# Two small edits to a fused attention and feed-forward kernel: another home for the parts of g, and a last result in two halves

## The chip, the cores and the metric

The kernel runs on one core of a Trainium2 chip. A core has five engines that run side by side, each with its own queue: TensorE (PE, matrix products, with a weight load shown as PEld), VectorE (DVE), ScalarE (ACT), GpSimd (POOL) and SyncE (SP, which here only issues DMA transfers). The metric is the device time of one execution in microseconds (us), the median of three runs.

## The reference

Attention over 8 batches, 8 heads, 576 positions and head size 64, with a local mask (32 wide) in four heads and a strided mask in the other four; its output, 4608 tokens by 512, goes through a feed-forward layer with softplus and 2048 inner columns. All in float32.

```python
attn = softmax(where(mask, q @ k.T / 8, -1e9))        # per batch and head
x = (attn @ v) laid out as (4608, 512)
h = x @ w_in                                          # (4608, 2048)
g = np.maximum(h, 0.0) + np.log1p(np.exp(-np.abs(h)))
out = g @ w_out                                       # (4608, 512)
```

## The kernel before

The feed-forward layer takes nearly all of the time. To keep float32 accuracy with PE's single-pass kind of float32 (`F32R`), each operand is kept as a rounded high part and a low part that holds the rest; a product is then three matmuls: high by high, high by low, low by high. So x is held as the tiles `x_h` and `x_l`, the inner activation g as `gh` and `gl`, and each weight tile `w_i` (of w_in) and `w_o` (of w_out) has both parts side by side.

The 4608 tokens are worked off in 9 chunks c of 512, and the 2048 inner columns in 16 steps f of 128. For each (c, f) there are two groups of PE work, of 12 matmuls each, every one 128x128 by 128x512:

- `hidden` (line 607): ph <- x, w_i. The stationary operand is a 128x128 cut of w_i, the moving one 512 columns of x_h or x_l. All 12 add up in one PSUM bank `ph`.
- `output` (line 647): py <- w_o, g. The stationary operand is a 128x128 cut of gh or gl, the moving one 512 columns of w_o. There are four results `py0` to `py3`, one for each 128 tokens of the chunk, with three matmuls each per step; they add up over the 16 steps.

Between the two stands the softplus: ACT makes u from ph (lines 619, 622, 624), DVE adds the positive part (L628), rounds u to gh (L256, in `copy_on`) and subtracts to get gl (L640). `output` runs two steps behind `hidden`, so PE alternates: 12 matmuls of ph, 12 of py, and so on. Where the attention of later batches comes due, its small matmuls (L328 scores, L484 weighted sums) are put between the groups. The first 130 us or so hold the loads, the preparation of the weights and the first attention pairs.

The order on every engine is fixed when the program is built: a list of names written by hand (`FIRST`) for the beginning, then a planner (`Plan`) that lays tasks on engines by costs and wished-for times. Buffers come from pools. Each pool gets a fixed stretch of the on-chip memory SBUF, in the order in which the pools are opened, and a tile has the same byte place in each of the 128 partitions. The pool `g` holds three buffers each for gh and gl, 2048 bytes per partition each; the pool `st` holds four small tiles for the softmax, 160 bytes each; `io` holds four buffers that the results o pass through on the way out.

At the end of a chunk `result` (lines 655 to 659) copies each py out of PSUM into an `io` buffer (py0 and py2 on ACT, py1 and py3 on DVE) and SP stores it with one DMA of 256 KB.

Of the kernel before, what the change touches and what calls it, by code (L numbers as in the profile page):

```python
# [9 lines left out]
F32 = mybir.dt.float32  # L10
# [9 lines left out]
P = 128  # L20
# [59 lines left out]
class Plan:  # L80
# [8 lines left out]
    def add(self, name, urgency, engine, cost, fn, after=(), late=0.0):  # L89
        self.tasks[name] = (urgency, len(self.tasks), engine, cost, fn, after, late)  # L90
# [29 lines left out]
def attention_softplus_ffn(  # L120
# [9 lines left out]
    nc = tc.nc  # L130
    B, NPAIR, _, _, S = qk.shape
    D = P // 2
    NT, DM = out.shape
    DFF = w_in.shape[1]
    NCC = DM // P
    NFC = DFF // P
# [9 lines left out]
    START = [sum(CH[:c]) for c in range(NCHUNK)]  # L146
    TPC = max(CH) // P

    const = ctx.enter_context(tc.tile_pool(name="const", bufs=1))
    x_pool = ctx.enter_context(tc.tile_pool(name="x", bufs=1))  # L150
    w_pool = ctx.enter_context(tc.tile_pool(name="w", bufs=1))
    st_pool = ctx.enter_context(tc.tile_pool(name="st", bufs=4))
    u_pool = ctx.enter_context(tc.tile_pool(name="u", bufs=2))
    g_pool = ctx.enter_context(tc.tile_pool(name="g", bufs=3))
    io_pool = ctx.enter_context(tc.tile_pool(name="io", bufs=4))
    ps_s = ctx.enter_context(tc.tile_pool(name="ps_s", bufs=1, space=bass.MemoryType.PSUM))
    ps_o = ctx.enter_context(tc.tile_pool(name="ps_o", bufs=1, space=bass.MemoryType.PSUM))
# [39 lines left out]
    py = [ps_y.tile([P, DM], F32, name=f"py{t}") for t in range(TPC)]  # L197
# [57 lines left out]
    def copy_on(engine, dst, src):  # L255
        (engine.copy if engine is nc.scalar else engine.tensor_copy)(dst, src)  # L256
# [167 lines left out]
    def prob_transposes(n, quarters=range(4)):  # L424
        p = prob[n % 2]
        for quarter in quarters:
            for place, h in (divmod(quarter, 2),):
                src = p[64 * place + 32 * h : 64 * place + 32 * h + 32]
                for lo, hi in ((0, 6), (6, 9)):
                    a, i = block_at(lo, place)  # L430
                    for c in range(2):
                        nc.vector.transpose(  # L432
                            pt[
                                32 * (i + c) : 32 * (i + c) + 32,
                                h,
                                a : a + hi - lo,
                                32 * i : 32 * i + 32,
                            ],
                            src[:, lo:hi, 32 * c : 32 * c + 32],
                        )  # L440
# [157 lines left out]
    def hidden(c, f, pairs=range(NPAIR)):  # L598
        n = CH[c]
        if 0 in pairs:  # L600
            phs[c, f] = ps_h.tile([P, 512], F32, tag="ph", name=f"ph_{c}_{f}")[:, :n]
        ph = phs[c, f]
        t0 = START[c] % RING
        i = 3 * pairs[0]
        for cc in (PAIRS[pair] for pair in pairs):
            for half, x in ((0, "h"), (1, "h"), (0, "l")):
                nc.tensor.matmul(  # L607
                    ph,
                    lhsT=w32["i", f][:, half, cc * P : (cc + 1) * P],
                    rhs=x_of(x, cc)[:, t0 : t0 + n],  # L610
                    start=(i == 0),
                    stop=(i == 3 * NCC - 1),
                )
                i += 1

    def log_part(c, f, steps=range(3)):
        if 0 in steps:
            us[c, f] = u_pool.tile([P, 512], F32, tag="u", name=f"u_{c}_{f}")[:, : CH[c]]
            nc.scalar.activation(us[c, f], phs[c, f], AF.Abs)  # L619
        u = us[c, f]  # L620
        if 1 in steps:
            nc.scalar.activation(u, u, AF.Exp, scale=-1.0)  # L622
        if 2 in steps:
            nc.scalar.activation(u, u, AF.Ln, bias=1.0)  # L624

    def softplus(c, f):
        u = us[c, f]
        nc.vector.scalar_tensor_tensor(  # L628
            u, in0=phs.pop((c, f)), scalar=0.0, in1=u, op0=ALU.max, op1=ALU.add
        )  # L630

    def g_high(c, f, engine=nc.vector):
        g = g_pool.tile([P, 512], F32R, tag="gh", name=f"gh_{c}_{f}")[:, : CH[c]]
        ghs[c, f] = g
        copy_on(engine, g, us[c, f])

    def g_low(c, f, engine):
        g = g_pool.tile([P, 512], F32R, tag="gl", name=f"gl_{c}_{f}")[:, : CH[c]]
        gls[c, f] = g
        engine.tensor_tensor(g, us.pop((c, f)), ghs[c, f].bitcast(F32), op=ALU.subtract)  # L640

    def output(c, f, ts=None):
        gh, gl = ghs[c, f], gls[c, f]
        for t in ts or range(CH[c] // P):
            sl = slice(t * P, (t + 1) * P)
            for n, (g, half) in enumerate(((gh, 0), (gh, 1), (gl, 0))):
                nc.tensor.matmul(  # L647
                    py[t],
                    lhsT=g[:, sl],
                    rhs=w32["o", f][:, half],  # L650
                    start=(f == 0 and n == 0),
                    stop=(f == NFC - 1 and n == 2),
                )

    def result(c, t, engine):
        o = io_pool.tile([P, DM], F32, tag="io", name=f"o_{c}_{t}")
        copy_on(engine, o, py[t])
        t0 = START[c] + t * P
        nc.sync.dma_start(out[t0 : t0 + P, :], o)

    idle = ps_s.tile([P, 512], F32, tag="ps", name="idle")

# [80 lines left out]
    for t in range(4):  # L743
        task(f"y{t}", result, 0, t, of(f"y{t}", (nc.scalar, nc.vector)[t % 2]))
# [19 lines left out]
    steps = [(c, f) for c in range(NCHUNK) for f in range(NFC)]  # L764
# [7 lines left out]
    def joint(i):  # L772
        return pair_at.get(i, 0) > 2 * NPAIR
# [3 lines left out]
    t = 0.0  # L777
# [6 lines left out]
    add = plan.add  # L784
# [6 lines left out]
    for i in range(begin, len(steps) + LAG):  # L791
        if i < len(steps):
            c, f = steps[i]
            w, x = CH[c] / 384, when[i]
            after = [f"F{i-1}", f"u{i-2}"] + wanted.get(c, [])
            if joint(i - 1):
                after.append(f"L{pair_at[i - 1] - 1}1")
            add(f"F{i}", x, "PE", 2.1 * w, lambda c=c, f=f: hidden(c, f), after)
            after = [f"F{i}", f"l{i-2}"]
            add(f"A{i}", x + 2, "ACT", 1.5 * w, lambda c=c, f=f: log_part(c, f), after)  # L800
            add(f"u{i}", x + 3.7, "DVE", 0.55 * w, lambda c=c, f=f: softplus(c, f), [f"A{i}"])
            after = [f"u{i}", f"O{i-3}"]
            add(f"h{i}", x + 4.1, "DVE", 0.35 * w, lambda c=c, f=f: g_high(c, f), after)
            after = [f"h{i}", f"O{i-3}"]
            add(f"l{i}", x + 4.3, "DVE", 0.55 * w, lambda c=c, f=f: g_low(c, f, nc.vector), after)
        k = i - LAG
        c, f = steps[k]
        w = CH[c] / 384
        x = when[i] + 2.1 * w
        nt = CH[c] // P  # L810
        if 0 < f < NFC - 1:
            add(f"O{k}", x, "PE", 2.1 * w, lambda c=c, f=f: output(c, f), [f"l{k}", f"O{k-1}"])
            continue
        before = f"O{k-1}"
        for t in range(nt):
            name = f"O{k}" if t == nt - 1 else f"O{k}.{t}"
            after = [f"l{k}", before] + ([f"y{k-1}.{t}"] if f == 0 else [])
            add(name, x + 0.01 * t, "PE", 0.7, lambda c=c, f=f, t=t: output(c, f, (t,)), after)
            before = name
            if f == NFC - 1:  # L820
                e, cost, engine = (("ACT", 0.5, nc.scalar), ("DVE", 0.6, nc.vector))[t % 2]
                fn = lambda c=c, t=t, engine=engine: result(c, t, engine)
                add(f"y{k}.{t}", x + 0.7 * t + 0.7, e, cost, fn, [name])
# [5 lines left out]
    for i, n in pair_at.items():  # L829
        x = when[i]  # L830
# [16 lines left out]
        y = x + 1.5  # L847
# [17 lines left out]
        for j in range(4):  # L865
            name = f"P{n}" if j == 3 else f"P{n}.{j}"
            fn = lambda n=n, j=j: prob_transposes(n, (j,))
# [6 lines left out]
        for half in range(2):  # L874
# [8 lines left out]
            fn = lambda n=n, half=half: x_part(n, half, False)  # L883
            add(f"H{n}{half}", z, "ACT", 0.35, fn, after)
            fn = lambda n=n, half=half: x_part(n, half, True)
# [82 lines left out]
```

## Time and profile before

| | |
|---|---|
| time, median of 3 runs | 913.67 us (913.51 to 913.80) |
| the profiled execution's own time | 914.04 us |
| its span, first to last instruction | 912.0 us |
| mean clock granted to PE | 0.999 |
| busy: PE, DVE, ACT, POOL | 900.4, 601.9, 446.3, 60.1 us |

The profiled execution is 0.37 us longer than the median, and 2.0 us of its time lie outside the span. A row of the chain of work ("pieces") gives a start, a duration and how many instructions were taken together. A row of the instructions in order of time gives start, duration, engine, line, operation, what is written and read, and in brackets the idle time before. Matmuls overlap, and the ends shown are modelled, so the pace of PE is read from starts: from one row's start to another's, divided by the matmuls that lie between.

### The profile page before, as it was taken

The page shows a single profiled execution, that of the slowest core. Times are in us where ns is not written, and L with a number is a line of the kernel's source. Part 1 is how long each engine was busy: PE and PEld are TensorE (multiplying, and loading weights), DVE is VectorE, ACT ScalarE, POOL GpSimd, SP SyncE. Part 2 cuts the span into 40 slices and gives each one's busy share as a digit, 9 for nine tenths or more (in the row PEclk, how much of TensorE's full clock was granted, in tenths as well). Part 3 has the DMA queues.
Part 4 walks back from the last instruction along what each step waited for, and adds up shares of the span by engine and source line. Part 5 has one row for each costly group of instructions (what it writes and reads, how often), then busy time and mean ns, then how long its engine had stood idle before and what let it go on. Part 6 is the DMA issues. An engine that isn't in the chain of part 4 may idle for free.

```text
span 912.0 us, 14487 instructions
## 1 busy us (share of the span) xinstructions
PE 900.4 (99%) x5700; PEld 725.3 (80%) x5700; DVE 601.9 (66%) x1308; ACT 446.3 (49%) x795; POOL 60.1 (7%) x77
## 2 busy tenths in 40 slices
PE   8899999999999999999999999999999999999998
PEld 5677778888888888888888888888888888888886
DVE  7999997877767667766766676776776333333332
ACT  7898855445444444444544444445443333333332
POOL 4343540000000000000000000000000000000000
PEclk9999999999999999999999999999999999999999
DMA  9927212122211112111211121111200010001001
GB/s 339 349 102 246 81 30 73 43 57 67 70 39 43 43 44 89 32 42 43 89 44 43 43 78 27 42 43 43 89 18 17 1 46 1 1 1 47 0 1 47
DMA packets 49939, 58.27 MB, mean 64 GB/s; under 512 B 3152, under 2 KB 35024, under 8 KB 49872
## 3 DMA queue, kind: packets, MB, share of 16 engines
q1 hardware_dynamic: 49728, 57.16, 19.5%
q8 instruction: 45, 0.74, 0.3%
q10 hardware_dynamic: 144, 0.20, 0.1%
q14 instruction: 22, 0.18, 0.1%
HBM read 47.91 MB, written 9.44 MB: 63 GB/s over the span
## 4 chain that ended last, share of the span: by engine, by line
PE 90%; DVE 6%; ACT 1%; DMA 1%; issue 1%; POOL 0%; SPq 0%; ACTq 0%; DVEq 0%; POOLq 0%
PE py L647 42%; PE ph L607 41%; PE ps L328 3%; PE pv L484 2%; PE po L484 1%; DVE pt L432 1%; PE po L328 1%; DVE u L628 1%; DMA kT<-in_qk_dram 1%; DVE a_o L561 1%; DVE a_i L561 0%; ACT prob L374 0%; DMA raw_q<-in_qk_dram 0%; DVE a_o L578 0%; DVE a_i L578 0%
## 5 line engine op out<-in xcount | busy, mean ns | idle before, releaser
L647 PE MATMUL py<-w_o,gh 128*128 128x512 f32 x1152 | 365.7, 398 | 0.0
L607 PE MATMUL ph<-x_h,w_i 128*128 128x512 f32 x1152 | 358.8, 392 | 0.4 <-DVE u L628 0.4
L619 ACT ACTIVATE u<-ph 128x512 f32<-128x512 f32 x144 | 86.3, 600 | 409.0 <-PE ph L607 409.0
L647 PEld LDWEIGHTS py<-w_o,gh 128*128 128x128 f32 x1152 | 214.4, 188 | 51.8 <-POOL w_o L593 0.9
L607 PEld LDWEIGHTS ph<-x_h,w_i 128*128 128x128 f32 x1152 | 215.8, 188 | 48.9 <-DVE u L628 0.9
L647 PE MATMUL py<-w_o,gl 128*128 128x512 f32 x576 | 227.1, 394 | 0.0
L607 PE MATMUL ph<-x_l,w_i 128*128 128x512 f32 x576 | 225.9, 392 | 0.0
L628 DVE SCALAR_TENSOR_TENSOR u<-ph,u 128x512 f32<-128x512 f32 x144 | 98.9, 688 | 181.0 <-ACT u L624 179.2
L432 DVE STREAM_TRANSPOSE pt<-prob 32x192 f32<-32x192 f32 x448 | 137.1, 314 | 6.4
L647 PEld LDWEIGHTS py<-w_o,gl 128*128 128x128 f32 x576 | 108.6, 189 | 25.7
L607 PEld LDWEIGHTS ph<-x_l,w_i 128*128 128x128 f32 x576 | 108.1, 188 | 25.3
L640 DVE TENSOR_TENSOR gl<-u,gh 128x512 fp32r<-128x512 f32 x138 | 96.1, 697 | 11.2 <-ACT gh L256 0.3
L622 ACT ACTIVATE u<-u 128x512 f32<-128x512 f32 x144 | 91.0, 632 | 4.5
L624 ACT ACTIVATE u<-u 128x512 f32<-128x512 f32 x144 | 90.8, 631 | 4.4
L256 ACT COPY qT<-prob 64x576 f32<-64x576 f32 x56 | 70.6, 1260 | 0.3
L256 DVE CAST gh<-u 128x512 fp32r<-128x512 f32 x130 | 55.4, 426 | 10.6 <-PE py L647 0.5
L391 DVE TENSOR_TENSOR prob<-ps,mask_b 128x384 f32<-128x384 f32 x24 | 13.4, 558 | 53.6 <-PE ps L328 53.6
L328 PEld LDWEIGHTS ps<-kT,qT 128*64 128x64 f32 x720 | 23.6, 137 | 11.7 <-issue 8.8
L328 PE MATMUL ps<-kT,qT 128*64 128x64 f32 x720 | 28.0, 226 | 0.3 <-ACT qT L256 0.3
L484 PE MATMUL pv<-pt,v_in 128*64 128x96 f32 x396 | 22.2, 248 | 0.0
L422 DVE TENSOR_TENSOR prob<-prob,st 128x576 f32<-128x576 f32 x28 | 21.2, 758 | 0.9
L391 DVE TENSOR_TENSOR prob<-po,mask_b 128x192 f32<-128x192 f32 x24 | 8.6, 358 | 19.3 <-ACT x_h L522 19.3
(89 smaller groups left out, 516.7 us busy)
## 6 DMA issues: line engine op xcount, KB each, us to landing
out_dram<-o SPq DMA_DIRECT2D x36, 256.0 KB, 2.2
v_in<-in_v_dram SPq DMA_DIRECT2D x28, 320.0 KB, 3.7
ri<-in_moe_w_in_dram SPq DMA_DIRECT2D x16, 512.0 KB, 7.2
ro<-in_moe_w_out_dram SPq DMA_DIRECT2D x16, 512.0 KB, 7.7
prob<-in_qk_dram SPq DMA_DIRECT2D x28, 288.0 KB, 2.8
kT<-in_qk_dram SPq DMA_DIRECT2D x28, 288.0 KB, 3.0
v_in<-in_v_dram SPq DMA_DIRECT2D x28, 48.0 KB, 2.8
room<-in_v_dram SPq DMA_DIRECT2D x4, 320.0 KB, 7.2
```

The source lines that it names most:

```text
L256: (engine.copy if engine is nc.scalar else engine.tensor_copy)(dst, src)
L328: nc.tensor.matmul(ps[64 * place : 64 * place + 64, 64 * (x - lo) : 64 * (x - lo) + 64], lhsT=blocks_of(n)[:, c // 32].rearrange("p h l -> ...
L391: nc.vector.tensor_tensor(pv, sv, m, op=ALU.add)
L432: nc.vector.transpose(pt[32 * (i + c) : 32 * (i + c) + 32, h, a : a + hi - lo, 32 * i : 32 * i + 32,], src[:, lo:hi, 32 * c : 32 * c + 32],)
L484: nc.tensor.matmul(po[64 * h : 64 * h + 64, TILE * x : TILE * x + TILE], lhsT=vs[n][:, a, h, :], rhs=pt_of(n, a)[:, h, a % 2], start=True, ...
L607: nc.tensor.matmul(ph, lhsT=w32["i", f][:, half, cc * P : (cc + 1) * P], rhs=x_of(x, cc)[:, t0 : t0 + n], start=(i == 0), stop=(i == 3 * N ...
L619: nc.scalar.activation(us[c, f], phs[c, f], AF.Abs)
L622: nc.scalar.activation(u, u, AF.Exp, scale=-1.0)
L624: nc.scalar.activation(u, u, AF.Ln, bias=1.0)
L628: nc.vector.scalar_tensor_tensor(u, in0=phs.pop((c, f)), scalar=0.0, in1=u, op0=ALU.max, op1=ALU.add)
L640: engine.tensor_tensor(g, us.pop((c, f)), ghs[c, f].bitcast(F32), op=ALU.subtract)
L647: nc.tensor.matmul(py[t], lhsT=g[:, sl], rhs=w32["o", f][:, half], start=(f == 0 and n == 0), stop=(f == NFC - 1 and n == 2),)
```

## The change

The pool `g` is opened first instead of after `u`. And the very last result, py3 of the last chunk, is copied in two halves of 256 columns: DVE takes the first, ACT the second. The first half is stored through SP as before, the second through ACT's own DMA queue. Since each call of `result` takes an `io` buffer, the last chunk now takes five of the four.

```diff
+    g_pool = ctx.enter_context(tc.tile_pool(name="g", bufs=3))
     const = ctx.enter_context(tc.tile_pool(name="const", bufs=1))
     x_pool = ctx.enter_context(tc.tile_pool(name="x", bufs=1))
     w_pool = ctx.enter_context(tc.tile_pool(name="w", bufs=1))
     st_pool = ctx.enter_context(tc.tile_pool(name="st", bufs=4))
     u_pool = ctx.enter_context(tc.tile_pool(name="u", bufs=2))
-    g_pool = ctx.enter_context(tc.tile_pool(name="g", bufs=3))
     io_pool = ctx.enter_context(tc.tile_pool(name="io", bufs=4))
...
-    def result(c, t, engine):
-        o = io_pool.tile([P, DM], F32, tag="io", name=f"o_{c}_{t}")
-        copy_on(engine, o, py[t])
+    def result(c, t, engine, cols=slice(0, DM)):
+        o = io_pool.tile([P, DM], F32, tag="io", name=f"o_{c}_{t}")[:, cols]
+        copy_on(engine, o, py[t][:, cols])
         t0 = START[c] + t * P
-        nc.sync.dma_start(out[t0 : t0 + P, :], o)
+        queue = nc.scalar if engine is nc.scalar and cols.start else nc.sync
+        queue.dma_start(out[t0 : t0 + P, cols], o)
...
-            if f == NFC - 1:
+            if k == len(steps) - 1 and t == nt - 1:
+
+                for h, (e, engine) in enumerate((("DVE", nc.vector), ("ACT", nc.scalar))):
+                    cols = slice(DM // 2 * h, DM // 2 * (h + 1))
+                    fn = lambda c=c, t=t, engine=engine, cols=cols: result(c, t, engine, cols)
+                    add(f"y{k}.{t}{h}", x + 0.7 * t + 0.7, e, 0.35, fn, [name])
+            elif f == NFC - 1:
```

What the first edit does to the byte places, as the two programs have them (first byte of a pool in each partition; the last two columns say where a place stands within 512 bytes):

| pool | before | after | before, modulo 512 | after, modulo 512 |
|---|---|---|---|---|
| g (gh and gl, 2048 bytes each) | 208768 | 256 | 384 | 256 |
| const | 256 | 12544 | 256 | 256 |
| x (x_h, x_l, 6144 bytes each) | 23808 | 36096 | 256 | 256 |
| w (w_i, w_o, 4096 bytes each) | 72960 | 85248 | 256 | 256 |
| st (four tiles, 160 bytes apart) | 204032 | 216320 | 256 | 256 |
| u | 204672 | 216960 | 384 | 384 |
| io | 221056 | 221056 | 384 | 384 |

All pools from const to u move up by 12288 bytes, which is 24 times 512. The cuts that PE reads start at multiples of 512 bytes within their tiles. The g buffers stood behind the four tiles of st, which take 640 bytes together, and so 128 bytes off the raster on which x and w stand; now they stand on it.

No engine's order changes before the last result. There, on ACT's queue, these are the last rows before the change (o are the `io` buffers, numbered by chunk and result; in brackets the counters waited for: DMAHW for a landed DMA, DVE, PE and Activation for engines):

```order
L624 ACTIVATE u_8_15_7852<-u_8_15_7852 128x512 [waits Activation_49]
L256 COPY o_8_0_7876<-py0_106 128x512 [waits DMAHW5_49,PE_49]
L256 COPY o_8_2_7888<-py2_108 128x512 [waits DMAHW7_49,DMAHW3_49,PE_49]
L963 UNCONDITIONAL_BRANCH
```

And these after it, from the same place on:

```order
L256 COPY o_8_0_7876<-py0_106 128x512 [waits DMAHW5_49,PE_49]
L256 COPY o_8_2_7888<-py2_108 128x512 [waits DMAHW7_49,DMAHW3_49,PE_49]
L256 COPY o_8_3_7897<-py3_109 128x256 [waits DMAHW1_49,DVE_49,Activation_49]
L660 DMA out_0_dram<-o_8_3_7897 128x256 [waits Activation_49]
L970 UNCONDITIONAL_BRANCH
```

ACT's half of py3 does not wait for PE. It waits for DVE, whose last counted work is the other half's copy, and for DMAHW1, the counter of the store of o_8_0, whose buffer it takes over.

SP's queue ends with these stores after the change; before, the last one was 128x512 and stood alone:

```order
L660 DMA out_0_dram<-o_8_0_7876 128x512 [waits DMAHW1_49,Activation_49]
L660 DMA out_0_dram<-o_8_1_7882 128x512 [waits DMAHW2_49,DVE_49]
L660 DMA out_0_dram<-o_8_2_7888 128x512 [waits DMAHW3_49,Activation_49]
L660 DMA out_0_dram<-o_8_3_7894 128x256 [waits DMAHW4_49,DVE_49]
L970 UNCONDITIONAL_BRANCH
```

The store of o_8_3 on SP has shrunk to half, and its other half has gone to ACT's queue.

## The prediction

> **What bounds the kernel now.** I read the page's engine line, then the chain of work that ended last, then the instructions in order of time.
>
> ```profile
> span 912.0 us, 14487 instructions
> PE 900.4 (99%) x5700; PEld 725.3 (80%) x5700; DVE 601.9 (66%) x1308; ACT 446.3 (49%) x795; POOL 60.1 (7%) x77
> ```
>
> PE is busy all the time, but matmuls overlap, so this says nothing of its pace. The chain from 129 us to the end is PE alone, but for a last copy; this is its row by line:
>
> ```profile
> by line: PE py L647 47.8%; PE ph L607 44.9%; PE ps L328 2.6%; PE pv L484 1.7%; PE po L484 1.5%; PE po L328 1.1%; DVE o L256 0.1%; issue 0.0%
> ```
>
> So whatever makes a py or ph matmul shorter there shortens the kernel by as much. How long is a group of 12? The chain around 715 us:
>
> ```profile
> 712.35 2.75 PE ph L607 x12
> 715.10 1.14 PE pv L484 x24
> 716.24 2.98 PE py L647 x12
> 719.22 2.73 PE ph L607 x12
> 721.95 2.80 PE py L647 x12
> 724.75 2.76 PE ph L607 x12
> 727.50 2.80 PE py L647 x12
> 730.30 2.76 PE ph L607 x12
> ```
>
> A py group takes 2.80, a ph group 2.76, though both have twelve matmuls of the same shape; and the ph group at 719 takes 2.73. The starts of PE's rows show where the difference lies:
>
> ```profile
> 719.06 0.62 PE L607 MATMUL ph<-x_h,w_i 128*128 128x512 f32 x2
> ...
> 721.10 0.62 PE L607 MATMUL ph<-x_h,w_i 128*128 128x512 f32 x2
> ...
> 721.79 0.64 PE L647 MATMUL py<-w_o,gh 128*128 128x512 f32 x2
> ...
> 724.58 0.62 PE L607 MATMUL ph<-x_h,w_i 128*128 128x512 f32 x2
> ...
> 725.27 0.62 PE L607 MATMUL ph<-x_h,w_i 128*128 128x512 f32 x2
> ...
> 725.97 0.62 PE L607 MATMUL ph<-x_h,w_i 128*128 128x512 f32 x2
> ...
> 726.65 0.62 PE L607 MATMUL ph<-x_h,w_i 128*128 128x512 f32 x2
> ```
>
> From 719.06 to 721.10 lie nine matmuls: 0.2267 us each, a clean pace. The twelve of py from 721.79 to 724.58 take 0.2325 each. The ph group behind them starts in the slow mode (0.69 and 0.70 for three) and gets to the clean pace later (0.68 for three from 725.97). At the clean pace twelve take 2.72. So a py group loses 0.08, and an ordinary ph group 0.04 at its start, by what py leaves behind.
>
> Why is py slow? Not by the neighbours: DVE worked in the clean stretch, as its rows in order of time show.
>
> ```profile
> 719.28 0.43 DVE L256 CAST gh<-u 128x512 fp32r<-128x512 f32 x1
> 719.74 0.69 DVE L640 TENSOR_TENSOR gl<-u,gh 128x512 fp32r<-128x512 f32 x1
> ```
>
> And in the last py groups both DVE and ACT stood idle from about 903.7 on; the rows of three engines, with the idle time before them in brackets:
>
> ```profile
> 903.68 0.62 PE L647 MATMUL py<-w_o,gh 128*128 128x512 f32 x2
> ...
> 905.77 0.64 PE L647 MATMUL py<-w_o,gh 128*128 128x512 f32 x2
> ...
> 905.97 0.59 ACT L256 COPY o<-py 128x512 f32<-128x512 f32 x1 [4.35 <-PE py L647]
> ...
> 906.67 0.69 DVE L256 COPY o<-py 128x512 f32<-128x512 f32 x1 [3.00 <-PE py L647]
> ```
>
> Nine matmuls in 2.09, 0.2322 each, with PE alone at work. Nor is it the change of PSUM bank after every third matmul, since ph, all in one bank, shows the same slow mode at 724.58. Nor the place of single w_o tiles: the groups at 721.95 and 727.50 read different ones at 2.80 each. What is left that all py have and no ph has: the stationary cuts come from g, which stands 128 bytes off the 512-byte raster on which x, w_i and w_o all stand. PE reads a moving stream and the next weights at once; I take it that the two disturb each other by where they lie relative to each other, that ph has a timing without disturbance into which it settles, and that py has none. This is inferred, not shown: no row has the same matmul with g elsewhere.
>
> **The change part by part.**
>
> *The home of g.* It removes and adds no instruction; no order and no wait differs before the last copy, and each engine's work on g stays as it was, if the byte place costs it nothing. x, w and u move by 24 rasters, so they stand to each other as before; only g's offset changes, to that of w_i. If this is the cause, py gets ph's clean pace, and ph has nothing to recover from. The groups that count, from the busy times by stretch (its bounds, its length, PE busy and matmuls, weight loads, clock, DMA), first those of L647, then of L607:
>
> ```profile
> 129.00:908.00 779.00, 392.96 (x1584) 296.26 (x1584) 1.00 0.14 41
> ```
>
> ```profile
> 129.00:908.00 779.00, 372.36 (x1530) 286.76 (x1528) 1.00 0.14 41
> ```
>
> In this stretch PE is the chain: 1584/12 = 132 py groups, 1530/12 = 127.5 ph groups. 25 py groups come behind attention matmuls (one is the 2.98 row: a stall, then the slow mode), from the planner's 24 pairs and the last sums. Terms: 107 ordinary py groups by 0.08 is 8.6; 25 py groups behind a stall by 0.05 is 1.3 (between 0 and 0.08; nearer the upper end, since only their first matmul is the stall's); 127.5 ph groups by 0.04 is 5.1. From this comes off the settling after each of the 25 stalls, priced like ph's after py: 25 by 0.04 is 1.0. Sum 14.0. Before 129 us DVE, ACT and loads are in the chain, so I count nothing there; the bounds are 0 and 12 py by 0.08 plus 16.5 ph by 0.04, or 1.6. The work that py's pace could uncover is DVE's: 66% busy, so two per cent less time is no bound. Bounds of the whole term: a gain of 15.0 + 1.6, and a loss if a new offset disturbed ph throughout as well: 127.5 by 0.04, or 5.1.
>
> Against this stands a rule of the Trainium skill, page "SBUF — State Buffer", section "Who interferes with whom": PE has two independent read ports, one for the moving operand and one for weight loads, and never waits on anyone. By that rule g's place would be worth 0 and the time would stay at 913.7. The 0.0058 us by which py's matmuls exceed ph's has no source in that rule, so I hold the trace against it; as a rival it stays.
>
> *The last result.* Before, the path ends: copy on DVE, issue by SP, landing, closing steps. Rows in order of time, then the row of the stores with their time to landing:
>
> ```profile
> 908.07 0.69 DVE L256 COPY o<-py 128x512 f32<-128x512 f32 x1 [0.70 <-PE py L647]
> ...
> 906.58 0.33 SPq L659 DMA_DIRECT2D out_dram<-o  x1
> ...
> 908.78 0.33 SPq L659 DMA_DIRECT2D out_dram<-o  x1
> ...
> out_dram<-o SPq DMA_DIRECT2D x4, 256.0 KB, 2.0
> ```
>
> The last store lands at 908.78 + 2.0 = 910.8; 1.2 later the span ends. After it, DVE's half is shorter; no row has 128x256, so I bound it by two DVE reads of PSUM, from the groups by shape:
>
> ```profile
> L391 DVE TENSOR_TENSOR prob<-ps,mask_b 128x384 f32<-128x384 f32 x24 | 13.4, 558 | 53.6 <-PE ps L328 53.6
> L391 DVE TENSOR_TENSOR prob<-po,mask_b 128x192 f32<-128x192 f32 x24 | 8.6, 358 | 19.3 <-ACT x_h L522 19.3
> ```
>
> A third of the way from 192 to 384 is 0.425: done at 908.49. ACT's half cannot run beside it: it waits for DVE's half and for the store of o_8_0, which is issued at 906.58 and lands at 908.6. ACT's copy of 256 columns lies between these:
>
> ```profile
> L522 ACT CAST x_h<-po 128x288 fp32r<-128x288 f32 x17 | 6.5, 382 | 0.0
> L522 ACT CAST x_h<-po 128x192 fp32r<-128x192 f32 x6 | 1.9, 309 | 0.0
> ```
>
> 0.36, so 908.65 to 909.0; issue at once, landing 2.0 later or up to 0.4 earlier for half the bytes: 910.65 to 911.05, against 910.8. The term is +0.05, between -0.15 and +0.25; were both halves free at 908.07, landing by 910.5, it would be -0.3. Nothing that a measurement could tell.
>
> *Sum.* 914.04 - 14.0 + 0.05 = 900.1 for the profiled execution; the median of the runs is 0.37 below it: 899.7. Since the settling may take more than I priced, I say 900.0.
>
> **Rivals.**
>
> 1. *The place of g is worth nothing* (the skill's rule, or a cause that I have not seen): the last result alone, 913.4 to 913.9. For it: no row shows the effect of an offset. Against it: nothing else sets py apart from ph.
> 2. *Every change between ph and py disturbs anew.* Then py becomes like an ordinary ph, 2.76, and ph stays: 132 by 0.04 is 5.3, time 908.4. For it: ph needs several matmuls to settle after py. Against it: the ph group at 719 starts clean straight behind py.
> 3. *On the other side: the new offset is worse.* If g's new place disturbs ph so that it never settles, its 127.5 groups take 2.80, 5.1 more: 918.8. The point that decides is whether ph reaches 0.68 for three matmuls before its twelfth. Against it: g then stands to w_o as w_i stands to x, the offset at which ph settles.
>
> **How the numbers follow.** My case 0.62, with its own range 897.5 to 903; rival 1 0.21; rival 2 0.12; rival 3 0.05. Faster by over 0.2% (1.8 us, about what a measurement can tell from no change): 0.62 + 0.12 = 0.74; within it 0.21; slower 0.05. My case and rival 2 hold less than 8 in 10, so the range reaches up over rival 1, to 914.2; at the lower end it takes in nearly all of the 16.6, at 897.5.
>
> **What the profile of the changed kernel would show.** Right: py groups in the chain at 2.72 to 2.73, ordinary ph groups too, three py matmuls from start to start in 0.68; the rows of attention unchanged; DVE's and ACT's rows on u, gh and gl at their durations. The last ACT copy starts some 0.6 behind the start of DVE's half, not with it, and from that start to the end of the span it is 3.9, as from 908.07 now. Wrong: py groups at 2.80 as now (rival 1), at 2.76 (rival 2), or ph groups at 2.80 (rival 3); or PE's groups shorter with new idle time ahead of them, by a wait on DVE for gl, which would say that I misjudged the slack.

## The result, and the profile after

| | before | after |
|---|---|---|
| time, median (4 runs each, side by side) | 913.59 us (912.82 to 913.80) | 899.68 us (899.59 to 899.95) |
| ratio after to before | | 0.9848, 95% interval 0.9834 to 0.9863 |
| the profiled execution's own time | 914.04 us | 899.74 us |
| its span | 912.0 us | 897.5 us |

The kernel is 13.9 us faster; 900.0 was said. The head of the page after the change, with the engines' busy times:

```profile
span 897.5 us, 14490 instructions
PE 885.0 (99%) x5700; PEld 723.8 (81%) x5700; DVE 601.4 (67%) x1308; ACT 446.9 (50%) x796; POOL 60.0 (7%) x77
```

The three instructions more are the second half of the last result: a copy, a DMA and what goes with them. PE is as full as before, at 15.4 us less. The chain of waits of the changed kernel from 129 to 900 us has nearly the same owners as before, PE with py and ph:

```profile
by line: PE py L647 47.1%; PE ph L607 44.9%; PE ps L328 2.6%; PE pv L484 1.7%; PE po L484 1.5%; PE po L328 1.1%; DMA out_dram<-o 0.3%; ACT o L256 0.1%; issue 0.0%; ACTq L256 0.0%
```

So it was not that a bound moved; PE's own groups became shorter. The same chain around 715 us (start, duration, what, how many matmuls), to be laid beside the rows of before in the prediction:

```profile
701.82 2.72 PE ph L607 x12
704.54 1.14 PE pv L484 x24
705.68 2.99 PE py L647 x12
708.67 2.72 PE ph L607 x12
711.39 2.72 PE py L647 x12
```

Every py and every ph group takes 2.72, except the py group behind the attention matmuls (pv, 24 of them), which holds a stall as before. PE's instructions in order of time show the pace by their starts:

```profile
716.66 0.62 PE L647 MATMUL py<-w_o,gh 128*128 128x512 f32 x2
...
717.34 0.62 PE L647 MATMUL py<-w_o,gh 128*128 128x512 f32 x2
...
718.02 0.62 PE L647 MATMUL py<-w_o,gh 128*128 128x512 f32 x2
...
718.70 0.62 PE L647 MATMUL py<-w_o,gh 128*128 128x512 f32 x2
...
719.38 0.62 PE L607 MATMUL ph<-x_h,w_i 128*128 128x512 f32 x2
```

Twelve py matmuls from 716.66 to 719.38: 2.72, or 0.2267 us each. That is the pace which only undisturbed ph groups had before. The costliest groups of the page, before:

```profile
L647 PE MATMUL py<-w_o,gh 128*128 128x512 f32 x1152 | 365.7, 398 | 0.0
L607 PE MATMUL ph<-x_h,w_i 128*128 128x512 f32 x1152 | 358.8, 392 | 0.4 <-DVE u L628 0.4
```

and after:

```profile
L647 PE MATMUL py<-w_o,gh 128*128 128x512 f32 x1152 | 359.2, 393 | 0.1
L607 PE MATMUL ph<-x_h,w_i 128*128 128x512 f32 x1152 | 355.7, 390 | 1.0 <-DVE u L628 1.0
L640 DVE TENSOR_TENSOR gl<-u,gh 128x512 fp32r<-128x512 f32 x138 | 96.1, 697 | 11.2 <-ACT gh L256 0.3
L256 DVE CAST gh<-u 128x512 fp32r<-128x512 f32 x130 | 55.4, 426 | 10.6 <-PE py L647 0.5
```

The mean of one py matmul fell by 5 ns, of one ph matmul by 2 ns, though of the distances between two operands only that of g and w_o, py's, has changed. Since the duration of an overlapped matmul is modelled, this points the right way and no more; the sizes are taken from starts. The two rows of DVE show that writing g at the new place takes as long as before (the page before has the same 697 and 426 ns).

The end, DVE and ACT in order of time:

```profile
893.66 0.42 DVE L256 COPY o<-py 128x256 f32<-128x256 f32 x1 [0.67 <-PE py L647]
894.38 0.37 ACT L256 COPY o<-py 128x256 f32<-128x256 f32 x1 [0.81 <-DMA out_dram<-o]
894.78 0.35 ACTq L660 DMA_DIRECT2D out_dram<-o  x1
```

ACT's half does not run beside DVE's: it starts 0.72 later, when the store named in the bracket has landed. From DVE's start at 893.66 to the end of the span it is 3.86; before, from 908.07 on, it was 3.91 (the spans to the hundredth are 897.52 and 911.98).

### The profile page after: what moved, and what is told of

It reads as the page before. It is cut to its first block, busy times and chain, and to the rows that moved or that the text cites. A ratio compares the mean times of both kernels' runs of the same rounds, so it can differ in the third digit from the quotient of the medians.

```text
span 897.5 us, 14490 instructions
## 1 busy us (share of the span) xinstructions
PE 885.0 (99%) x5700; PEld 723.8 (81%) x5700; DVE 601.4 (67%) x1308; ACT 446.9 (50%) x796; POOL 60.0 (7%) x77
## 4 chain that ended last, share of the span: by engine, by line
PE 86%; DVE 6%; ACT 3%; DMA 3%; issue 1%; SPq 1%; POOL 0%; ACTq 0%; POOLq 0%
PE py L647 40%; PE ph L607 39%; PE ps L328 2%; DMA ri<-in_moe_w_in_dram 2%; PE pv L484 2%; DVE pt L432 1%; PE po L484 1%; PE po L328 1%; ACT qT L256 1%; ACT prob L374 1%; DVE u L628 1%; DMA ro<-in_moe_w_out_dram 1%; DVE a_i L561 1%; DVE a_o L561 0%; DVE a_o L578 0%
## 5 line engine op out<-in xcount | busy, mean ns | idle before, releaser
L647 PE MATMUL py<-w_o,gh 128*128 128x512 f32 x1152 | 359.2, 393 | 0.1
L647 PE MATMUL py<-w_o,gl 128*128 128x512 f32 x576 | 224.2, 389 | 0.0
```

Of the source, the lines that this page charges most:

```text
L647: nc.tensor.matmul(py[t], lhsT=g[:, sl], rhs=w32["o", f][:, half], start=(f == 0 and n == 0), stop=(f == NFC - 1 and n == 2),)
```

## The experiments

Theory A, that of the prediction: PE reads the moving stream and the next stationary cut from SBUF at once, and the pace depends on the distance of the two within some raster. Its variant A2: what counts is the place of g within the raster, not its distance from w_o. Rival R: the region counts, since the change also brought g to the front of SBUF. A rival from the other half of the change: the last result has a share in the gain. And a question within A: is the raster 512 bytes, or 256? Each diff is against the changed kernel, except where it says against the one before. A line number can be up to four higher than in the listing above. All were timed against the kernel before in the same session; its medians there were 913.1 to 913.4 us.

**Which half of the change.** Against the kernel before, g's pool alone is moved (e4), and the halves alone are made (e8, with the hunks on `result` and on the last step shown in the change).

```diff
+    g_pool = ctx.enter_context(tc.tile_pool(name="g", bufs=3))
     const = ctx.enter_context(tc.tile_pool(name="const", bufs=1))
...
-    g_pool = ctx.enter_context(tc.tile_pool(name="g", bufs=3))
```

> Only the move of g; the last result is copied and stored whole, as in the kernel before. If the halves are worth between -0.15 and +0.25 us as forecast, this is at 899.5 to 899.9, and from the start of the last copy on DVE to the end of the span it is 3.93 us as in the kernel before, against 3.83 in the changed kernel. A theory by which the halves bring the gain: 913.6.

Measured: 899.76 us, ratio 0.9853 (0.9838 to 0.9867).

> The kernel before with the last result in two halves, g at its old place. From the changed kernel against the one with g moved alone the halves are worth about -0.1 us: the last store lands 0.1 later, and the closing steps are 0.2 shorter. So 913.3 to 913.7, no difference that can be measured. py at 2.80, ph at 2.76. A theory by which the halves need g's move, or bring it: anything under 912.

Measured: 913.08 us, ratio 0.9996 (0.9986 to 1.0006). The whole gain that can be measured is g's place; the halves make no difference that this measurement can tell. The traces show how little they can be worth: from the start of DVE's last copy to the end of the span it is 3.79 to 3.87 us in all twelve traces with the halves, and 3.91 and 3.93 in the two without (the kernel before and e4).

**Place or region.** g's pool goes behind w, to byte 204032, far from the front but on the raster.

```diff
-    g_pool = ctx.enter_context(tc.tile_pool(name="g", bufs=3))
...
     w_pool = ctx.enter_context(tc.tile_pool(name="w", bufs=1))
+    g_pool = ctx.enter_context(tc.tile_pool(name="g", bufs=3))
```

> The pool of g stands at the upper end again, right behind w (first byte 204032 instead of 256 in the changed kernel), but on the same 512-byte raster as x and w (256 modulo 512). All else is the changed kernel. Theory A, the offset of the weights that PE loads against the stream that it reads (modulo 512) makes py slow: as the changed kernel, 899.7 us, py groups of 12 matmuls at 2.72. Theory B, the upper region of the memory makes py slow: as before, about 913.6, py groups at 2.80 and ph groups at 2.76.

Measured: 899.62 us, ratio 0.9855 (0.9840 to 0.9870), all ordinary groups (those not next to attention matmuls) at 2.72:

```profile
716.35 2.72 PE py L647 x12
719.07 2.72 PE ph L607 x12
```

R falls: 4.7 KB below its old place g is as good as at the front. Now the reverse, in front but 128 bytes off, with two small tiles put ahead of g:

```diff
+    front = ctx.enter_context(tc.tile_pool(name="front", bufs=1))
     g_pool = ctx.enter_context(tc.tile_pool(name="g", bufs=3))
...
-    kT = [const.tile([P, PAD + S], F32, name=f"kT_{i}") for i in range(2)]
+    kT = [(front, const)[i].tile([P, PAD + S], F32, name=f"kT_{i}") for i in range(2)]
...
-    ident_b = const.tile([P, P], BF16, name="ident_b")
+    ident_b = front.tile([P, P], BF16, name="ident_b")
```

> g stays at the front of the memory, but kT_0 and ident_b (2688 bytes) are put ahead of it, so that it begins at 2944, which is 384 modulo 512: 128 bytes off the raster of x and w, as in the kernel before. x, w and u stand where the changed kernel has them. Theory A (offset): about 913.6, py at 2.80, ph at 2.76. Theory B (region): 899.7, py at 2.72.

Measured: 913.70 us, ratio 1.0006 (0.9997 to 1.0015). The chain of this kernel is the old one again, the recovering ph group behind the stall included:

```profile
717.04 2.98 PE py L648 x12
720.02 2.73 PE ph L608 x12
722.74 2.80 PE py L648 x12
725.54 2.76 PE ph L608 x12
```

In front, too, 128 bytes of offset give the whole loss back.

**Distance or place.** st's pool is opened first, so that g, x, w_i and w_o all stand at 384 modulo 512, each 128 off the old raster.

```diff
+    st_pool = ctx.enter_context(tc.tile_pool(name="st", bufs=4))
     g_pool = ctx.enter_context(tc.tile_pool(name="g", bufs=3))
...
-    st_pool = ctx.enter_context(tc.tile_pool(name="st", bufs=4))
```

> The pool st (640 bytes) is opened first, so that g, x and w all stand 128 bytes further on (384 modulo 512) and 0 against each other. Theory A, in the form that the distance between weights and stream counts: 899.7, py and ph at 2.72. Theory A2, in the form that weights must stand at 256 modulo 512 by themselves, wherever the stream is: py at 2.80 and ph at 2.80 too, since w_i is off as well; 918 or more. Theory B (region): 899.7.

Measured: 899.78 us, ratio 0.9855 (0.9838 to 0.9871), all ordinary groups at 2.72:

```profile
716.87 2.72 PE py L647 x12
719.59 2.72 PE ph L607 x12
```

g is where it was bad, modulo 512, and is good since w_o is there too. A2 falls; the distance counts. Nor is it the distance of g to u, which ACT and DVE work on: both stand at 384 in this fast kernel, as both did in the slow one before.

**Is it a trait of py?** Now w_i and w_o go 128 up, x and g stay. Then py is 128 off again, the other way round, and ph gets a distance for the first time, the one that py had in the kernel before: there w_i is the stationary operand and x moves.

```diff
+    st_pool = ctx.enter_context(tc.tile_pool(name="st", bufs=4))
     w_pool = ctx.enter_context(tc.tile_pool(name="w", bufs=1))
-    st_pool = ctx.enter_context(tc.tile_pool(name="st", bufs=4))
```

> Changed kernel with st (640 bytes) opened between x and w: w_i and w_o stand at 384 modulo 512, x and g at 256. The distance that py had in the kernel before (weights 128 behind the stream) now belongs to ph: weights from w_i, stream from x. py gets weights 128 ahead of the stream, as in the run with kT_0 ahead of g. Theory A (distance of the two operands): ph groups at 2.80 throughout, never settling; with py at 2.80 as well if both senses are bad, then about 918.8; if only the first sense is bad, py recovers what ph leaves behind and the time is near 913. A theory by which py is slow for another reason than distance (its PSUM banks, its operands being g and w_o): ph at 2.72, 899.7.

Measured: 918.31 us, ratio 1.0054 (1.0037 to 1.0070). Its chain:

```profile
704.19 2.80 PE py L647 x12
706.99 2.80 PE ph L607 x12
709.79 2.80 PE py L647 x12
```

ph is as slow as py and never settles: rival 3's picture, and near its 918.8. So the effect is no trait of py, g or w_o: both pairs of stationary and moving operand that this kernel has show it.

**The raster.** First g lies 256 from the others modulo 512, since only `ident_b`, 256 bytes, goes ahead of it:

```diff
+    front = ctx.enter_context(tc.tile_pool(name="front", bufs=1))
     g_pool = ctx.enter_context(tc.tile_pool(name="g", bufs=3))
...
-    ident_b = const.tile([P, P], BF16, name="ident_b")
+    ident_b = front.tile([P, P], BF16, name="ident_b")
```

> Changed kernel, but ident_b (256 bytes) is put ahead of g: g begins at 512, so weights from g and the stream from w_o are 256 bytes apart modulo 512 (128 in the kernel before, 0 in the changed one). x, w, u as in the changed kernel. Theory P512, only a distance of 0 modulo 512 is good: about 913.6, py at 2.80. Theory P256, the raster is 256: 899.7, py at 2.72.

Measured: 899.82 us, ratio 0.9847 (0.9832 to 0.9861), all ordinary groups at 2.72:

```profile
716.56 2.72 PE py L648 x12
719.28 2.72 PE ph L608 x12
```

Then 128 below them, with only kT_0 ahead of g (2432 bytes):

```diff
+    front = ctx.enter_context(tc.tile_pool(name="front", bufs=1))
     g_pool = ctx.enter_context(tc.tile_pool(name="g", bufs=3))
...
-    kT = [const.tile([P, PAD + S], F32, name=f"kT_{i}") for i in range(2)]
+    kT = [(front, const)[i].tile([P, PAD + S], F32, name=f"kT_{i}") for i in range(2)]
```

> Changed kernel, but kT_0 (2432 bytes) is put ahead of g: g begins at 2688, 128 modulo 512, so its weights stand 128 bytes ahead of the stream's place modulo 512 (384 in the other sense), where the kernel before had them 128 behind. If each distance other than the raster is bad: about 913.6, py at 2.80. If only one side is bad, for the weight load and the stream run after each other in one sense: 899.7, py at 2.72.

Measured: 913.49 us, ratio 1.0000 (0.9991 to 1.0010), py at 2.79 and 2.80, ph at 2.76. A distance of 256 is as good as none, and 128 is as bad below as above: as far as these distances tell, the raster is 256 bytes.

**Smaller distances.** An unused tile of 64, 32 or 96 bytes stands between g and all the rest, so that g lies so far below the others.

```diff
     g_pool = ctx.enter_context(tc.tile_pool(name="g", bufs=3))
+    pad = ctx.enter_context(tc.tile_pool(name="pad", bufs=1))
+    pad.tile([P, 64], U8, name="pad")
```

> Changed kernel with 64 empty bytes between g and const: x and w stand at 320 modulo 512, g at 256, so g's weights are 64 bytes off the stream. ph as before (w_i and x move together). If the disturbance grows with the distance from the raster: between 899.7 and 913.6, near 906, py at 2.76. If 64 bytes are a raster of their own: 899.7. If any distance is as bad as 128: 913.6.

Measured: 903.74 us, ratio 0.9890 (0.9874 to 0.9907). py loses little, ph nothing:

```profile
717.29 2.72 PE ph L609 x12
720.01 2.75 PE py L649 x12
```

> Changed kernel with 32 empty bytes between g and const: x and w stand at 288 modulo 512, g at 256. So far the distance costs a py group 0 at 0 and 256 bytes, 0.027 us at 64 and 0.076 at 128. If the cost grows evenly with the distance up to 128: half of 64's, 0.013, by 132 groups 1.8 us, 901.5. If 64 bytes are a step (half a raster) and everything below it is free: 899.7. If any distance but 0 and 256 costs at least as much as 64: 903.7 or more.

Measured: 909.19 us, ratio 0.9953 (0.9939 to 0.9968): slower than at 64.

```profile
717.59 2.79 PE py L649 x12
720.38 2.73 PE ph L609 x12
```

> Changed kernel with 96 empty bytes between g and const: x and w at 352 modulo 512, g at 256. If the cost grows evenly up to 128: a py group at 2.72 + 0.05 = 2.77, and if ph has to settle after it as at 128, 0.04 more per ph group; without that 906.5, with it 911. If the cost goes in steps of 64: as at 64, 903.7.

Measured: 915.38 us, ratio 1.0026 (1.0016 to 1.0036): slower than at 128, which none of the expectations had.

```profile
722.53 2.80 PE py L649 x12
725.33 2.77 PE ph L609 x12
728.09 2.80 PE py L649 x12
```

The cost does not grow evenly with the distance. In the kernels with 32 and 96, x, w_i and w_o stand at places that 64 does not divide, which could have been a second cause. So a last one has the distance of 32 again, but with g on such a place (288) and the others on a multiple of 64 (320):

```diff
+    pad0 = ctx.enter_context(tc.tile_pool(name="pad0", bufs=1))
+    pad0.tile([P, 32], U8, name="pad0")
     g_pool = ctx.enter_context(tc.tile_pool(name="g", bufs=3))
+    pad1 = ctx.enter_context(tc.tile_pool(name="pad1", bufs=1))
+    pad1.tile([P, 32], U8, name="pad1")
```

> In the kernel with g 32 under, g stood on a place divisible by 64 (256 modulo 512) and x, w_i and w_o on one that is not (288). Here the distance is the same, 32, but g stands at 288 and x, w_i and w_o at 320. If only the distance counts: 909.2 again, py groups at 2.79, ph at 2.73. If in that kernel the moving stream's own place off a raster of 64 made py slow: 899.7, all groups at 2.72. If a stationary cut's place off that raster is what costs: also about 909, but the next ph group need not show the same clean start; this run cannot tell it from the first by the time alone.

Measured: 909.69 us, ratio 0.9958 (0.9945 to 0.9972), with the rows of 32 again:

```profile
717.51 2.79 PE py L651 x12
720.31 2.73 PE ph L611 x12
723.03 2.79 PE py L651 x12
```

Which of the two stands off a multiple of 64 makes no difference, and ph, with both its operands on odd places in the earlier kernel, had its clean starts there. It is the distance once more. The form of the curve stays open. What each distance does is seen best from the time between starts of successive py matmuls, in ns, worked out from the traces for one ordinary group of each kernel between 717 and 730 us (0 is the changed kernel, 128 the one before):

```
  0   227 227 226 227 227 226 227 227 226 227 227 226
 32   233 234 231 235 233 235 230 235 234 234 231 226
 64   229 232 226 229 232 225 230 231 226 229 232 227
 96   232 237 231 232 237 231 232 237 231 232 237 229
128   241 232 231 232 228 230 233 240 233 231 231 234
```

The last number of a row leads over to ph. At 64 the excess comes in a pattern of three, at 96 too, at 128 in one of seven or so. And as a rule only at 96 and 128 does py leave ph in a slow mode: at 32 and 64 the next ph group runs at 226 to 227 from its first matmul on. There are exceptions behind the stalls of attention: three ph groups start slow at 64, and two start clean at 128, the one at 719.06 in the prediction among them.

Which two reads belong together shows at the borders between groups. These are two borders in the kernel with 32, from py to ph and from ph to py (PEld is the weight load):

```profile
719.99 0.39 PE L649 MATMUL py<-w_o,gl 128*128 128x512 f32 x1
720.00 0.41 PEld L609 LDWEIGHTS ph<-x_h,w_i 128*128 128x128 f32 x2
720.22 0.62 PE L609 MATMUL ph<-x_h,w_i 128*128 128x512 f32 x2
...
722.71 0.40 PE L609 MATMUL ph<-x_l,w_i 128*128 128x512 f32 x1
722.72 0.42 PEld L649 LDWEIGHTS py<-w_o,gh 128*128 128x128 f32 x2
722.95 0.63 PE L649 MATMUL py<-w_o,gh 128*128 128x512 f32 x2
```

The weights of the next matmul are loaded while the one before it streams. py's last matmul moves w_o while the first cut of w_i is loaded; both stand at 288, and the spacing is 226 ns (the rows round it to hundredths of a us). ph's last moves x at 288 while the first cut of g is loaded, from 256, and the spacing is 235, at every such border of this kernel; with g at 288 and the rest at 320 it is 235 again, and 236 to 237 at a distance of 96. So what counts is the moving operand of one matmul against the stationary cut of the next, as theory A has it. At 64 the borders say nothing: there every third spacing within py is clean, and so is the one from ph to py (225 to 226).

## Why the prediction was right, step by step

The mechanism and each large term held. Sums over all groups from 129 us on, from start to next start in the two traces (26 groups behind attention instead of the 25 that I counted):

| term | predicted | measured | from |
|---|---|---|---|
| ordinary py groups | 8.6 | 7.9 | 106 groups; 102 of them went from 2.796 to 2.720 each |
| ph groups | 5.1 | 4.7 | 1527 matmuls, 353.13 to 348.41 us |
| py groups behind attention | 1.3 - 1.0 = 0.3 | 1.0 | 26 groups, 75.20 to 74.19 us |
| attention matmuls | 0 | 0.0 | 53.38 to 53.37 us |
| before 129 us | 0, up to 1.6 | 0.7 | the py group with which these sums begin starts at 128.75 instead of 129.48 |
| last result | -0.05, between -0.25 and 0.15 | 0.1 | 3.91 to 3.86 us to the end of the span |
| sum | 14.0 | 14.4 | of 14.5 in the span |

That the sum came so close is in part luck, since its errors went against each other: the first two terms were 1.1 too high, and the groups behind attention and the stretch before 129 us 1.4 too low. The 0.3 by which 900.0 stands above the sum's 899.7 was put there for a longer settling, and the settling was shorter. The upper bound of 15.0 counts the groups behind a stall at 0.05, though the text allows them 0.08; with that it would be 15.7.

*py's pace.* Rightly read from starts. The cost of one group is 0.076, not 0.08; rows rounded to hundredths of a us gave the rest.

*ph's recovery.* Predicted from a slow start behind py, and gone with it; e9 shows the other side, that ph itself can be held in the slow mode all the time. One thing was put in the wrong place: of the 4.7, only 4.1 lie in the slow starts of the groups. The other 0.6 lie in the last spacing of each, 232 to 233 ns before and 226 to 227 after, where the first cut of g is loaded.

*The raster.* The prediction counted places modulo 512, and its change brought the distance to 0 by either count. e5 shows that 256 would have done as well.

*Settling.* This was mis-sized. For each group behind a stall I counted a gain of 0.05 and took 0.04 off again, in the belief that PE settles behind a stall as slowly as ph did behind py; that made 0.3 in all, and these groups gave 1.0. The starts of a typical one (behind attention at 634.14 us) lie 337, 236, 228, 232, 231, 227 ns apart, and from there on at 226 or 227. After the stall itself its eleven spacings take 2.514 us, 0.021 above the clean pace. Before the change such a group (at 643.44 us) had 2.557, 0.064 above it. So the gain was 0.064 and the settling 0.021: both terms were off, in the same direction. Settling needs no offset: at distance 0 the py group behind attention at 705.61 us, the slowest of the 26, runs through 236, 224, 231, 236, 228, 233, 231 before it is clean, the very spacings with which a ph group behind py began before the change (at 657.45 us).

*Before 129 us.* Nothing was counted, and 0.7 came. PE has a part in that chain too, as the bounds allowed.

*DVE as the next bound.* It did not show. Idle time ahead of ph, waiting for u, rose from 0.4 to 1.0 us in the rows of the groups above.

*The last result.* ACT's half waits as told. DVE's half takes 0.42 as estimated from two other shapes, ACT's 0.37 for 0.36. It starts 0.72 after DVE's, not 0.6, and the stores land like this (the DMA issues of the changed kernel's last stretch, with the median time to landing):

```profile
out_dram<-o SPq DMA_DIRECT2D x1, 128.0 KB, 2.0
out_dram<-o ACTq DMA_DIRECT2D x1, 128.0 KB, 1.7
```

Half the bytes land in 2.0 on SP's queue, as 256 KB do, and in 1.7 on ACT's, within the bounds. So the split could gain next to nothing (0.05 us here), since its second half could only begin when the store of another result had landed; e8 gives the same verdict by the time.

*Rival 1* rested in part on the Trainium skill, page "SBUF — State Buffer", section "Who interferes with whom", by which PE reads its moving operand and its weights through independent ports and waits for no one. The measurement differs from what was drawn from it and decides: the same matmuls in the same order take 0.2267 or up to 0.233 us by the distance of those two operands alone. *Rival 2* (2.76 for both) and *rival 3* (2.80 for ph) would have shown in the rows above, and did not in the changed kernel.

What is not shown is why the two reads of PE disturb each other at some distances. No run looks into where they meet, and neither the 256 bytes nor the uneven curve between 0 and 128 is derived from anything.

## What to carry to other kernels

Where PE is the bound, look at the time from start to start of equal matmuls: if one kind is a few ns slower than another of the same shape, compare the byte places of its stationary and its moving operand modulo 256. In this kernel's 128x128 by 128x512 float32 matmuls, equal places cost nothing and 32 to 128 bytes apart cost 1% to 3% per matmul; only multiples of 32 were tried. A small pool of odd size (here four tiles of 160 bytes) shifts all that is opened behind it, so it belongs behind the operands of PE, or filled up to a multiple of 256.

## What the runs showed of the hardware that was not expected

- The pace of PE depends on the distance between stationary and moving operand modulo 256 bytes, not 512 as the prediction's raster had it: 899.7 us at 0 and 899.8 at 256, 913.5 to 913.7 at 128 on either side.
- It is not even in between: 909.2 and 909.7 us at 32, 903.7 at 64, 915.4 at 96. The nearer place is not the better one.
- A slow py group of 12 leaves the following ph matmuls slow, though their own operands are well placed, for some seven matmuls, at distances of 96 and 128 and, but for three groups behind attention, not at 32 and 64. This carry-over made up 4.1 of the 14.4 us.
- The distance that counts is that of the moving operand of one matmul to the stationary cut of the next, which is loaded meanwhile: 235 ns against 226 at the two kinds of border with g 32 off.
